# A two-stage attention kernel: the first part's order written out as one list, and the masks of stage 2 made early

## The chip, the core and the metric

The kernel runs on one core of a Trainium2 chip. The time is device time in microseconds (us), the slowest core of an execution, here the only one. A profiled execution is one more run, with the hardware profiler on; its span goes from the first to the last instruction of the core.

## What is computed

`reference.py`, cut to what matters. Two attentions follow each other, and the output of the first, regrouped by token, is the input of the second:

```python
# stage 1: q, k, v are (8 batches, 8 heads, 576 tokens, 64)
mask = (rel >= 0) & (rel < 64)                  # rel = query position - key position
attn = softmax(where(mask, q @ k.T / 8, -1e9))
x = (attn @ v), heads side by side: (8, 576, 512)
# stage 2: 4 experts, each a causal attention with 64 columns; 2 of 4 chosen per token
logits = x @ w_gate; keep the two largest, softmax over these two -> w
out = sum over the experts e kept of  w_e * (softmax(causal(x wq_e (x wk_e).T / 8)) @ (x wv_e)) @ wo_e
```

All arrays are f32. The products with the weights are formed from two reduced-precision parts (a high and a low one, names ending in `hi` and `lo`, `xh` and `xl`), three matmuls for one.

## The kernel before

**Stage 1.** Heads are taken in pairs `p`, 32 in all, four to a batch. A pair has nine blocks of 64 queries, and each block sees two blocks of 64 keys. Four blocks make a group `g`, so there are 72 groups, nine to a batch. For a group the steps are these:

- `s1_mm` (L201): scores on TensorE (PE) for two groups at once, 32 small matmuls, into two banks of PSUM (tag `s`, five banks). Text and names below call the call for groups 6 and 7 `m6`, and so on.
- `s1_qk`: the window mask and the row minimum on VectorE (DVE, L223), the exponentials on ScalarE (ACT, L231), then "norm": an add and a reciprocal on DVE (L238, L239) and four multiplications on GpSimd (POOL, L242), which leave the tile `sm`.
- `s1_t`: four transposes on PE (L262) for each group into a bank of PSUM (tag `t`, three banks), then the "evict", a copy of the bank to `pt` by ACT (L270) or DVE (L268). From group 18 on it is two groups to a bank, and DVE multiplies with a triangle (`tri`, L282) while it copies.
- `s1_av` (L303): 32 matmuls with `v` into a bank of tag `t`, whose result goes out as `xh` (ACT, L315) and `xl` (DVE, L317).

Text below writes t_3 for the transposes of group 3, sm_3 for its tile, o_3 for the 32 matmuls that end with group 3.

**Stage 2**, per batch: `s2_v` (`v2ps`, five products, with the copy of the logits at L415), the key and query projections (`kps`, `qps`; the matmuls are L384 to L386), the scores (L521), a masked softmax (DVE L542, ACT L546), transposes (L606, and L628 for the tile `px`, in the same three banks `t`), the product with `v` (L667), the output product (`ops`) and its copies (L710). It needs constants: `causal` and `m_f` (masks), `QF`, `V2` and `below` (tiles that must be cleared), all made in `stage2_constants`. The weights are loaded by `load_weight` and cut in two by `split_weights` (POOL the high part, DVE the low one).

**Loads** are all issued by SyncE (SP): `load_pair` (L86, L87) brings `q` and `k` of a pair, `load_v` (L99) brings `v`, each with three buffers; for pair 3 `q`, `k` and `v` go to the tiles `P2` (printed as `p`).

**What sets the order.** Every engine works off its instructions in the order in which they were emitted. Each step has a time on a scale of batches, and a heap hands the steps out by it. Steps with a time below `EARLY` (1.0) are emitted phase by phase: a step that yields goes back into the heap with a `DELAY` added. In this first part the order on PE, DVE, ACT and POOL is as emitted. After it, up to a time of 15.5, PE alone is held to the emitted order, and a scheduler of the framework orders the others; the order on SP is the framework's throughout.

Of the kernel before, what the change touches and what calls it, by code (L numbers as in the profile page):

```python
# [20 lines left out]
E = 4  # L21
DM = NH * D
NEG = -1.0e9
MERGE = 1
LPOS = (-2.607, -1.75, -1.7, -1.032, -2.6)
EARLY = 1.0
TPOS = 0.667
EPOS = {'V': (-0.113, 0.691), 'G': (1.179, 0.889), 'KQ0': (0.544, 0.987), 'KQ1': (-0.225, 0.85)}
ELAG = (0.453, 0.719)
EQ = (0.041, 0.024, 0.109, -0.306, -0.038, -0.309, 0.065, 0.065, -0.032, 0.149, 0.044, -0.017, -0.056, -0.019, -0.04, -0.032, -0.134, -0.038)  # L30
ET = (0.023, 0.156, -0.265, 0.001, 0.065, -0.095, 0.275, 0.092, 0.073, -0.065, 0.19, 0.023, 0.204, -0.256, 0.124, -0.171, -0.135, -0.241)
EV = (-0.045, 0.508, 0.147, 0.282, 0.083, 0.211, -0.168, 0.146, 0.096, 0.061, 0.442, 0.055, 0.456, 0.018, 0.112, -0.053, -0.034, -0.252)
DELAY = {'ttr': 0.008, 'exp': 0.04, 'norm': 0.193, 'evict': -0.227, 'xh': -0.02, 'xl': 0.181, 'v': 0.087, 'k': 0.008, 'lo': 0.343}
MM0 = 0.07
MORE = 0.0
MERGED = ()
MPOS = (0.091, 0.05)
WHOLE = ('sA1yb0xkt','sA1yb0xCkt')
LAG = (-0.048, 0.009, 0.29)
POS = {'T00': (-0.096, 0.044), 'T01': (-0.139, -0.078), 'T10': (0.181, 0.783), 'T11': (0.226, 0.424), 'T1l': (0.283, 0.638), 'O0': (0.161, 0.571), 'O1': (1.027, 0.988), 'KQ1': (-0.098, 0.991), 'V': (-0.003, 0.559), 'G': (0.685, 0.902), 'KQ0': (0.636, 0.932), 'VT': (-0.056, 0.001), 'T00e': (-0.05, 0.0), 'T10e': (0.096, 0.082), 'T01e': (-0.758, -0.894), 'T11e': (-0.421, -0.074), 'O0e': (0.418, 0.518), 'O1e': (0.851, 0.917)}  # L40
SPREAD = 'APAP'
LEAD = 12.49
FIXED = (1.0, 15.5)
WPOS = [-0.711, -0.311, 0.131, 0.616]
CPOS = 0.058
JOIN8 = 1
JOIN = 2
BPOS = ((0.044, 0.828), (0.147, 0.721), (0.08, 0.3, 0.203), (-0.511, 0.073))
# [10 lines left out]
def window_attention_moe_attention(ctx: ExitStack, tc: tile.TileContext, qT, kT, vW,  # L59
                                   wg, wq, wk, wv, wo, out):  # L60
    nc = tc.nc
# [10 lines left out]
    def need(*keys):  # L72
        assert made.issuperset(keys), keys
# [76 lines left out]
    raws = {}  # L150
# [94 lines left out]
    def s1_t(g):  # L245

        k = g % 9
        if k % 2 == 0 and k != 8:
            return
        gs = [g - 1, g] if k % 2 else [g]  # L250
        need(*(("p1", y) for y in gs))
        if k == 8 and g // 9 >= JOIN and JOIN8:
            t = work.tile([128, 2, 2, 128], F32, tag="pt8", bufs=1, name=f"pt1_{g}")
        else:
            t = work.tile([128, 4, 2, 128], F32, tag="pt1", bufs=2, name=f"pt1_{g}")
        if g < FIRST:
            banks = []
            for x, y in enumerate(gs):
                pt = P1.pop(y)
                ps = psum.tile([128, 4, 128], F32, tag="t", bufs=3, name=f"t1_{y}")  # L260
                for i in range(4):
                    nc.tensor.transpose(ps[:, i], pt[:, i], ident)  # L262
                banks.append(ps)
            yield "evict"
            for x, ps in enumerate(banks):
                dst = t[:, 2 * x:2 * x + 2].rearrange("r a e c -> r (a e) c")
                if gs[x] % 2 and gs[x] < 9:
                    nc.vector.tensor_copy(dst, ps)  # L268
# [60 lines left out]
    L = [const.tile([128, 5, E], F32, name=f"logits{i}") for i in range(2)]  # L329
# [5 lines left out]
    V2 = [const.tile([128, 5, E, D], F32, name=f"v2_{i}") for i in range(2)]  # L335
# [15 lines left out]
    def stage2_constants():  # L351
        made.add("late")
        nc.vector.memset(m_f, 0.0)
        for h in range(2):
            r = slice(64 * h, 64 * h + 64)
            nc.gpsimd.affine_select(out=m_f[r, 0:64], in_=m_f[r, 0:64], pattern=[[-1, 64]],
                                    base=0, channel_multiplier=1, compare_op=OP.is_ge, fill=NEG)

        nc.gpsimd.memset(causal, 0.0)
        for c in (0, 640):  # L360
            nc.gpsimd.memset(causal[0:64, c:c + 64], -NEG)
            nc.vector.tensor_scalar(causal[64:128, c:c + 64], m_f[64:128, 0:64], -1.0, None, op0=OP.mult)
        for c in (64, 576):
            nc.vector.tensor_scalar(causal[0:64, c:c + 64], m_f[0:64, 0:64], -1.0, None, op0=OP.mult)
        nc.vector.tensor_scalar(m_f[:, 64:128], m_f[:, 0:64], -1.0, None, op0=OP.mult)
        for t in QF:
            nc.gpsimd.memset(t, 0.0)
        for t in V2:
            for e in range(E):
                nc.gpsimd.memset(t[64 - 64 * (e % 2):128 - 64 * (e % 2), 4, e], 0.0)  # L370
        nc.gpsimd.memset(below, 0.0)
        for e in range(1, E):
            nc.gpsimd.memset(below[:, e, 0:e], 1.0)

# [346 lines left out]
    def half(n):  # L721
# [75 lines left out]
    todo = [x for n in range(2 * NB + 2) for x in half(n)]  # L797
    joined = {}
    places = []
    for n in range(1, 2 * NB + 2):  # L800
# [4 lines left out]
        for x in range(3 if n == 2 * NB else 2):  # L805
            t = n + BPOS[n - 2 * NB + 2 if n >= 2 * NB else (n + 1) % 2][x]
# [3 lines left out]
    for g in range(NG1):  # L810
        t = (g - LEAD - MORE * min(max(g - 9, 0) / 27, 1)) / 4.5 + LAG[0]
        a, c = (ELAG if t < EARLY - 0.5 else (2 / 4.5 + LAG[1], 3 / 4.5 + LAG[2]))
        if g < 18:
            t, a, c = t + EQ[g], a + ET[g] - EQ[g], c + EV[g] - EQ[g]
        base = t
        if g < SOLO:
            todo.append((t - 1e-4, s1_mm, ((g,),)))
        elif g % 2 == 0:
# [3 lines left out]
            if at_burst:  # L822
                t = places.pop(0)
# [16 lines left out]
    todo.append((CPOS, stage2_constants, ()))  # L840
    todo.append((max(WPOS[:3]) + DELAY['lo'] + 1e-3, clear_pt2, ()))
    todo += [(LPOS[i], load_weight, (i,)) for i in range(4)]
    todo += [(LPOS[4] + 1e-3 * p, load_v, (p,)) for p in (2, 3)]
    todo.append((-99, first_constants, ()))
    todo.append((TPOS, tri_constants, ()))

    def steps(f, args):
        r = f(*args)
        if r is not None:
            yield from r  # L850

    order = [(x[0], i, steps(*x[1:])) for i, x in enumerate(todo)]
    heapq.heapify(order)
    E_ = mybir.EngineType
    for t1, engines in ((EARLY, {E_.PE, E_.DVE, E_.Activation, E_.Pool}), (FIXED[0], None), (FIXED[1], {E_.PE}), (99, None)):
        with tc.manual_schedule(engines=engines) if engines else nullcontext():
            while order and order[0][0] < t1:
                t, i, unit = heapq.heappop(order)
                for phase in unit:
                    if t < EARLY:  # L860
                        heapq.heappush(order, (t + DELAY[phase], len(todo) + i, unit))
                        break


# [52 lines left out]
```

## Time and profile before

| | us |
|---|---|
| median of three runs (483.93, 484.5, 555.47) | 484.5 |
| profiled execution | 487.01 |
| its span | 485.0 |
| PE busy | 464.4 (96%) |
| DVE busy | 390.3 (80%) |
| ACT busy | 339.2 (70%) |
| POOL busy | 210.3 (43%) |
| mean granted clock of PE | 0.987 |

A busy share is an average over the whole span. The first part, the first 60 us or so, differs from the rest: there the loads from memory are the densest, and the idle time of PE is at its largest. The first part goes from the first score matmul to the first scores of stage 2 at 58.07 us; after it come eight batches of stage 2, among which the remaining groups of stage 1 are spread.

### The profile page before, as it was taken

The numbers are of one execution on the slowest core, as the hardware profiler recorded it, in microseconds if no ns is written. First come the engines' busy times: TensorE is split into PE (matmuls) and PEld (weight loads), VectorE is DVE, ScalarE is ACT, GpSimd is POOL, SyncE is SP. The second block draws the span as 40 slices with busy tenths as digits, with TensorE's granted clock in tenths as the row PEclk, the third lists the DMA queues.
The fourth block names the chain that finished last, engine by engine and source line by source line (L and its number), as shares of the span: only waits on it lengthen the run. The fifth ranks groups of instructions, "written<-read, shape, count | busy, mean of one in ns | idle before, by whom it ended". The sixth has DMA issues, their size and how long they took to land.

```text
span 485.0 us, 15973 instructions
## 1 busy us (share of the span) xinstructions
PE 464.4 (96%) x5728; PEld 416.3 (86%) x5728; DVE 390.3 (80%) x1758; ACT 339.2 (70%) x1349; POOL 210.3 (43%) x559
## 2 busy tenths in 40 slices
PE   6899999999999999999999999999899999999996
PEld 5678888997899898897889989898789989999875
DVE  3596789899978998888988998888997896646473
ACT  4796698948677874867668786576867785557480
POOL 3479955624254353441636244361436333242120
PEclk8799999999999999999999999999999999999999
DMA  8982243321623134123522214333240101200103
GB/s 275 389 300 85 89 144 110 103 82 47 220 97 103 51 123 130 64 98 102 201 90 88 91 49 173 118 101 102 78 141 23 51 1 47 66 2 23 66 2 108
DMA packets 20926, 51.36 MB, mean 106 GB/s; under 512 B 2800, under 2 KB 3824, under 8 KB 20848
## 3 DMA queue, kind: packets, MB, share of 16 engines
q1 hardware_dynamic: 20768, 50.22, 30.7%
q8 instruction: 45, 0.74, 0.7%
q14 instruction: 33, 0.27, 0.2%
q10 hardware_dynamic: 80, 0.13, 0.1%
HBM read 40.90 MB, written 9.44 MB: 104 GB/s over the span
## 4 chain that ended last, share of the span: by engine, by line
PE 46%; DVE 30%; ACT 17%; issue 4%; POOL 1%; DMA 1%; DVEq 0%; ACTq 0%; SPq 0%; POOLq 0%
DVE pt L282 8%; ACT p L231 6%; PE o L667 6%; ACT p L546 5%; PE o L303 4%; PE s L521 4%; PE s L201 4%; DVE sm L223 4%; DVE p L542 4%; PE t L606 4%; PE ops L386 2%; PE ops L384 2%; PE ops L385 2%; PE qps L384 2%; PE t L262 2%
## 5 line engine op out<-in xcount | busy, mean ns | idle before, releaser
L586 POOL TENSOR_SCALAR p<-p,r 128x192 f32<-128x192 f32 (+3 forms) x124 | 74.8, 620 | 86.8 <-DVE r L581 66.1
L546 ACT ACTIVATE p<-p,r 128x192 f32<-128x192 f32 (+3 forms) x128 | 77.3, 606 | 44.7 <-DVE r L566 31.6
L242 POOL TENSOR_SCALAR p<-p,st 128x64 f32<-128x64 f32 x216 | 64.4, 323 | 81.4 <-DVE st L239 57.5
L231 ACT ACTIVATE p<-p,st 128x64 f32<-128x64 f32 x216 | 72.8, 339 | 30.7 <-DVE p L228 16.8
L282 DVE TENSOR_TENSOR pt<-t,tri 64x512 f32<-64x512 f32 (+1 forms) x120 | 76.0, 634 | 2.0
L601 ACT ACTIVATE pt<-t 128x512 f32<-128x512 f32 (+3 forms) x185 | 66.5, 386 | 7.3 <-PE t L628 4.3
L223 DVE CUSTOM_DVE_ANT_0 sm<-s,win 128x128 f32<-128x128 f32 x264 | 62.8, 284 | 6.7 <-PE s L201 6.3
L542 DVE CUSTOM_DVE_ANT_0 p<-s,causal 128x320 f32<-128x320 f32 (+3 forms) x160 | 66.9, 471 | 0.9
L606 PE MATMUL t<-ident,p 128*128 128x128 f32 x384 | 55.3, 275 | 4.7 <-ACT pt L601 3.7
L606 PEld LDWEIGHTS t<-ident,p 128*128 128x128 f32 x384 | 43.7, 141 | 9.6 <-ACT pt L601 5.7
L667 PE MATMUL o<-pt,v 128*64 128x128 f32 (+3 forms) x896 | 51.1, 263 | 0.0
L201 PE MATMUL s<-k,q 64*64 64x128 f32 (+1 forms) x1116 | 43.7, 281 | 6.0 <-DVE st L238 2.6
L667 PEld LDWEIGHTS o<-pt,v 128*64 128x64 f32 x896 | 46.2, 137 | 2.0 <-issue 0.8
L201 PEld LDWEIGHTS s<-k,q 64*64 64x64 f32 x1116 | 33.4, 138 | 13.1 <-issue 5.8
L521 PE MATMUL s<-kt,qt 64*128 64x256 f32 (+2 forms) x480 | 44.4, 321 | 0.0
L303 PEld LDWEIGHTS o<-pt,v 128*64 128x64 f32 x1116 | 35.9, 140 | 6.3 <-issue 2.0
L303 PE MATMUL o<-pt,v 128*64 128x64 f32 x1116 | 40.4, 227 | 0.8 <-DVE pt L268 0.8
L231 ACT ACTIVATION_READ_ACCUMULATOR p<-p,st 128x1 f32 x216 | 40.8, 189 | 0.0
L384 PE MATMUL qps<-xh,wqhi 128*128 128x320 f32 (+1 forms) x128 | 40.5, 316 | 0.0
L384 PE MATMUL v2ps<-wvhi,xh 128*128 128x260 f32 x128 | 39.0, 304 | 1.6 <-DVE logits L415 1.0
L384 PE MATMUL kps<-xh,wkhi 128*128 128x320 f32 (+1 forms) x128 | 39.3, 307 | 0.0
L521 PEld LDWEIGHTS s<-kt,qt 64*128 64x128 f32 x480 | 34.6, 185 | 4.4 <-issue 0.4
(138 smaller groups left out, 1190.9 us busy)
## 6 DMA issues: line engine op xcount, KB each, us to landing
v<-in_vW_dram SPq DMA_DIRECT2D x31, 576.0 KB, 4.8
k<-in_kT_dram SPq DMA_DIRECT2D x30, 320.0 KB, 3.9
q<-in_qT_dram SPq DMA_DIRECT2D x30, 288.0 KB, 3.1
out_dram<-out SPq DMA_DIRECT2D x32, 256.0 KB, 2.0
out_dram<-out SPq DMA_DIRECT2D x7, 128.0 KB, 2.3
p<-in_vW_dram SPq DMA_DIRECT2D x1, 576.0 KB, 8.0
pt<-in_wv_dram SPq DMA_DIRECT2D x1, 512.0 KB, 9.1
pt<-in_wk_dram SPq DMA_DIRECT2D x1, 512.0 KB, 7.4
```

The source lines that it names most:

```text
L201: nc.tensor.matmul(S1[g][i][o:o + 64, c:], lhsT=q_t[r, 64 * b:64 * b + 64], rhs=k_t[r, 64 * b + c:64 * b + 128], start=True, stop=True)
L223: nc.vector.tensor_tensor_reduce(out=to, in0=ps[i][:, c:], in1=win[:, int(b == 0), c:], scale=-0.125, scalar=3.0e38, op0=OP.add, op1=OP.mi ...
L231: nc.scalar.activation(pt[:, i], pt[:, i], AF.Exp, bias=st[:, 0, z + i:z + i + 1], scale=-1.0, accum_out=st[:, 1, z + i:z + i + 1])
L282: nc.vector.tensor_mul(t[64 * w:64 * w + 64, :n, e], ps[r, :n], tri[r, w, None, :].to_broadcast([64, n, 128]))
L303: nc.tensor.matmul(o[64 * h:64 * h + 64, 4 * x + i], lhsT=pairs[p][2][:, h, b], rhs=t[:, i, c:c + 64], start=True, stop=True)
L384: nc.tensor.matmul(ps, lhsT=ah, rhs=bh, start=first, stop=False)
L521: nc.tensor.matmul(banks[e][:, at(i, e):at(i, e) + n], lhsT=QT[pr][r, w, q], rhs=rhs, start=x == 0, stop=x == 2)
L542: nc.vector.tensor_tensor_reduce(out=dst, in0=ps, in1=mask, scale=1.0, scalar=3.0e38, op0=OP.add, op1=OP.min, accum_out=to)
L546: nc.scalar.activation(p, p, AF.Exp, bias=r2[:, 0, x:x + 1], scale=-1.0, accum_out=r2[:, 1, x:x + 1])
L586: engine.tensor_scalar(p, p, r2[:, 3, x:x + 1], 1.0, op0=OP.mult, op1=OP.mult)
L606: nc.tensor.transpose(ps[:, col:col + 128], P2S[pr][part][:, at:at + 128], ident)
L667: nc.tensor.matmul(o[64 * h:64 * h + 64, q0:q0 + w], lhsT=V2[b % 2][:, c, 2 * pr + h], rhs=PT2[part][:, h, x:x + w], start=a == 0, stop=a ...
```

## The change

The steps below time 1.0 are no longer handed out by the heap. A string `ORDER` lists them by short names, and each occurrence of a name emits the next phase of that step on all four engines: `m` is `s1_mm`, `q` `s1_qk`, `t` `s1_t`, `a` `s1_av`, `l` and `L` the loads of weights and of `v`, `w` `split_weights`, `v`, `k`, `r` the first projections of stage 2, `f`, `c`, `d`, `e`, `i`, `z` the constants. `stage2_constants` (`c`) keeps `m_f` and `causal` alone; `clear_stage2` (`d`) has the rest but for the second `V2`, which `clear_v2` (`e`) clears later. `ECOPY` says which groups' banks DVE copies: group 3's goes from DVE to ACT. Some numbers of the tables `TPOS`, `EPOS` and `POS` change as well, which moves a few steps after the first part. No step is added or left out.

```diff
...
-CPOS = 0.058
+WPOS = (-0.711, -0.211, 0.131, 0.616)
+CPOS = (-1.5, -1.4, 0.7)
+ECOPY = (0, 1, 0, 0, 0, 1, 0, 1, 0, 0, 0, 0, 0, 0, 0, 0, 0, 0)
...
+ORDER = (
+    'f m0 q0 q0 q0 l0 L2 m1 q1 q0 q1 t0 q1 m2 q1 q2 q3 a0 t2 q2 L3 q2 q3 q3 t1 q2 m4 t1 q3 q5 q4 q4 q4 t3 '
+    'q5 c a1 l2 q4 q5 t3 a2 t4 a1 m6 q6 m8 q6 q5 l1 a1 t5 q6 q7 q7 q7 q6 t5 a3 a3 a4 q7 q8 d q8 a3 q8 l3 '
+    'a6 m10 q9 q9 q9 q8 t6 t7 t7 q10 a5 a5 q10 t8 t8 t9 q11 q10 a7 a7 a8 a8 w0 q9 a5 w0 q10 a7 w1 q11 a8 '
...
-POS = {'T00': (-0.096, 0.044), 'T01': (-0.139, -0.078), 'T10': (0.181, 0.783), 'T11': (0.226, 0.424), 'T1l': (0.283, 0.638), 'O0': (0.161, 0.571), 'O1': (1.027, 0.988), 'KQ1': (-0.098, 0.991), 'V': (-0.003, 0.559), 'G': (0.685, 0.902), 'KQ0': (0.636, 0.932), 'VT': (-0.056, 0.001), 'T00e': (-0.05, 0.0), 'T10e': (0.096, 0.082), 'T01e': (-0.758, -0.894), 'T11e': (-0.421, -0.074), 'O0e': (0.418, 0.518), 'O1e': (0.851, 0.917)}
+POS = {'T00': (-0.096, 0.053), 'T01': (-0.139, -0.078), 'T10': (0.181, 0.783), 'T11': (0.226, 0.424), 'T1l': (0.283, 0.638), 'O0': (0.161, 0.571), 'O1': (1.027, 0.955), 'KQ1': (-0.098, 0.991), 'V': (-0.003, 0.559), 'G': (0.684, 0.813), 'KQ0': (0.636, 0.963), 'VT': (-0.037, 0.001), 'T00e': (-0.05, 0.0), 'T10e': (0.096, 0.082), 'T01e': (-0.758, -0.894), 'T11e': (-0.421, -0.074), 'O0e': (0.418, 0.518), 'O1e': (0.851, 0.917)}
...
-                if gs[x] % 2 and gs[x] < 9:
+                if ECOPY[gs[x]]:
                     nc.vector.tensor_copy(dst, ps)
...
         nc.vector.tensor_scalar(m_f[:, 64:128], m_f[:, 0:64], -1.0, None, op0=OP.mult)
+
+    def clear_stage2():
         for t in QF:
             nc.gpsimd.memset(t, 0.0)
-        for t in V2:
-            for e in range(E):
-                nc.gpsimd.memset(t[64 - 64 * (e % 2):128 - 64 * (e % 2), 4, e], 0.0)
         nc.gpsimd.memset(below, 0.0)
         for e in range(1, E):
             nc.gpsimd.memset(below[:, e, 0:e], 1.0)
+        clear_v2(0)
+
+    def clear_v2(x):
+        assert x == 0 or not {"o"} & set(raws)
+        for e in range(E):
+            nc.gpsimd.memset(V2[x][64 - 64 * (e % 2):128 - 64 * (e % 2), 4, e], 0.0)
...
-    for t1, engines in ((EARLY, {E_.PE, E_.DVE, E_.Activation, E_.Pool}), (FIXED[0], None), (FIXED[1], {E_.PE}), (99, None)):
+    with tc.manual_schedule(engines={E_.PE, E_.DVE, E_.Activation, E_.Pool}):
+        for x in ORDER.split():
+            next(units[x], None)
+    for t1, engines in ((FIXED[0], None), (FIXED[1], {E_.PE}), (99, None)):
         with tc.manual_schedule(engines=engines) if engines else nullcontext():
             while order and order[0][0] < t1:
-                t, i, unit = heapq.heappop(order)
-                for phase in unit:
-                    if t < EARLY:
-                        heapq.heappush(order, (t + DELAY[phase], len(todo) + i, unit))
-                        break
+                for phase in heapq.heappop(order)[2]:
+                    pass
```

The first place is DVE after the copy of `pt_1`, about 13 us into the span. `st_3` is what the norm of group 3 works on, `sm_4` and `sm_5` are the mask steps of groups 4 and 5. Before:

```order
43 L268 COPY pt_1_248<-t_1_254 128x512
44 L223 ISA sm_4_284,st_4_283<-s_4_0_261,win 128x128
...
51 L223 ISA st_4_283 128x1
52 L238 TENSOR_SCALAR st_3_232<-st_3_232 128x4
53 L239 RECIPROCAL st_3_232<-st_3_232 128x4
54 L223 ISA sm_5_300,st_5_299<-s_4_0_261,win 128x128
```

With the change:

```order
43 L277 COPY pt_1_242<-t_1_248 128x512
44 L247 TENSOR_SCALAR st_3_232<-st_3_232 128x4
45 L248 RECIPROCAL st_3_232<-st_3_232 128x4
46 L232 ISA sm_4_290,st_4_289<-s_4_0_259,win 128x128
...
61 L232 ISA st_5_310 128x1
62 L362 MEMSET m_f 128x128
63 L371 TENSOR_SCALAR causal<-m_f 64x64 x2
64 L373 TENSOR_SCALAR causal<-m_f 64x64 x2
65 L374 TENSOR_SCALAR m_f<-m_f 128x64
66 L247 TENSOR_SCALAR st_4_289<-st_4_289 128x4
67 L248 RECIPROCAL st_4_289<-st_4_289 128x4
```

The norm of group 3 has moved ahead of sm_4's eight instructions, and the mask instructions of stage 2, which stood behind the split of `wk`, now stand between sm_5 and the norm of group 4. On POOL their partners stand between sm_3 and sm_4, and the clearing of `qf`, `below` and the first `V2` between sm_7 and sm_8.

The second place is PE after t_3. Before:

```order
29 L262 MATMUL t_3_322<-ident,sm_3_233 128x128 x4
30 L201 MATMUL s_6_0_336<-k_84,q_83 64x128 x2
...
38 L303 MATMUL o_1_370<-pt_1_248,v_81 64x64 x16
39 L262 MATMUL t_4_389<-ident,sm_4_284 128x128 x4
40 L262 MATMUL t_5_394<-ident,sm_5_300 128x128 x4
41 L303 MATMUL o_3_418<-pt_3_316,v_81 64x64 x2
42 L303 MATMUL o_3_418<-pt_3_316,v_87 64x64 x14
43 L201 MATMUL s_8_0_438<-p_0_67,p_1_68 64x128 x2
```

With the change:

```order
29 L271 MATMUL t_3_305<-ident,sm_3_233 128x128 x4
30 L312 MATMUL o_1_333<-pt_1_242,v_81 64x64 x16
31 L210 MATMUL s_6_0_364<-k_84,q_83 64x128 x2
...
39 L210 MATMUL s_8_0_386<-p_0_67,p_1_68 64x128 x2
...
47 L271 MATMUL t_4_419<-ident,sm_4_290 128x128 x4
48 L271 MATMUL t_5_424<-ident,sm_5_311 128x128 x4
49 L312 MATMUL o_3_451<-pt_3_299,v_81 64x64 x2
```

o_1 has gone ahead of m6, and m8 (`s_8`) from behind o_3 to ahead of t_4. The second half of m8 reads pair 4. On SP the load of pair 3's `v` (576 KB) goes from ahead of pair 4's `q` and `k` to behind them.

The third place is PE in each batch of stage 2, at the query projection of the second half (`qps_0_1`). Before:

```order
467 L606 MATMUL t_0_1_0_1_1953<-ident,p_0_67 128x128 x4
468 L384 MATMUL qps_0_1_1961<-xh_863,wqhi 128x256
469 L385 MATMUL qps_0_1_1961<-xl_864,wqhi 128x256
...
479 L386 MATMUL qps_0_1_1961<-xh_863,wqlo 128x256
480 L628 MATMUL t_0_1_0_2_1976<-ident,px 128x128
```

With the change:

```order
467 L620 MATMUL t_0_1_0_1_1953<-ident,p_0_67 128x128 x4
468 L642 MATMUL t_0_1_0_2_1961<-ident,px 128x128
469 L398 MATMUL qps_0_1_1965<-xh_890,wqhi 128x256
470 L399 MATMUL qps_0_1_1965<-xl_891,wqhi 128x256
...
480 L400 MATMUL qps_0_1_1965<-xh_890,wqlo 128x256
```

One transpose, that of `px`, has gone ahead of the twelve matmuls of the projection. It writes a bank of tag `t` that the triangle step (L282) on DVE read last.

## Rows read from the trace of the kernel before

**Rows 1.** The page: busy time of two engines, their share, instructions.
```profile
PE 464.4 (96%) x5728; PEld 416.3 (86%) x5728; DVE 390.3 (80%) x1758; ACT 339.2 (70%) x1349; POOL 210.3 (43%) x559
```

**Rows 2.** What PE waited for, 0 to 62 us: total, times, longest.
```profile
PE s L201 <- DVE st L238: 2.6, 1, 2.6
PE t L262 <- POOL sm L242: 1.4, 2, 1.2
...
PE v2ps L384 <- DVE logits L415: 1.0, 1, 1.0
PE o L303 <- DVE pt L268: 0.8, 1, 0.8
PE t L262 <- DVE xl L317: 0.4, 1, 0.4
```

**Rows 3.** Stretches: length, busy us per engine, granted PE clock, DMA share, GB/s.
```profile
18.00:20.00 2.00, 2.00 (x37) 1.55 (x39) 1.24 (x4) 1.11 (x5) 1.60 (x5) 0.68 1.05 396
20.00:22.00 2.00, 2.00 (x34) 1.88 (x33) 0.86 (x8) 1.74 (x9) 1.11 (x4) 0.50 1.04 402
```

**Rows 4.** PE's timeline: start, us, line, tiles, count, [idle before, releaser].
```profile
16.93 1.37 PE L262 MATMUL t<-ident,sm 128*128 128x128 f32 x4 [1.21 <-POOL sm L242]
...
19.73 1.97 PE L303 MATMUL o<-pt,v 128*64 128x64 f32 x32
...
25.84 1.15 PE L303 MATMUL o<-pt,v 128*64 128x64 f32 x32
...
30.23 0.88 PE L262 MATMUL t<-ident,sm 128*128 128x128 f32 x4
```

**Rows 5.** DVE's timeline around the norm of group 3 and the masks.
```profile
13.12 0.66 DVE L268 COPY pt<-t 128x512 f32<-128x512 f32 x1
15.11 0.29 DVE L223 CUSTOM_DVE_ANT_0 sm<-s,win 128x128 f32<-128x128 f32 x1 [1.33 <-PE s L201]
...
15.96 0.16 DVE L238 TENSOR_SCALAR st<-st 128x4 f32<-128x4 f32 x1
16.16 0.18 DVE L239 RECIPROCAL st<-st 128x4 f32<-128x4 f32 x1
...
42.56 0.62 DVE L362 TENSOR_SCALAR causal<-m_f 64x64 f32<-64x64 f32 x2 [3.51 <-POOL causal L359]
...
43.41 0.18 DVE L365 TENSOR_SCALAR m_f<-m_f 128x64 f32<-128x64 f32 x1
```

**Rows 6.** ACT's timeline: the end of group 3's exponentials.
```profile
14.14 0.19 ACT L231 ACTIVATION_READ_ACCUMULATOR sm<-sm,st 128x1 f32 x1
```

**Rows 7.** POOL's timeline: groups 3 and 4, and the stage 2 constants.
```profile
16.50 2.80 POOL L242 TENSOR_SCALAR sm<-sm,st 128x128 f32<-128x128 f32 x8 [1.72 <-DVE st L239]
...
41.25 0.53 POOL L356 TENSOR_SCALAR_AFFINE_SELECT m_f<-m_f 64x64 f32<-64x64 f32 x2
...
42.76 0.34 POOL L367 MEMSET qf<- 128x128 f32 x2
43.16 1.45 POOL L370 MEMSET v<- 64x64 f32 x8
```

**Rows 8.** Loads of `k` issued from 13 to 16 us, and how long until landing.
```profile
L87 SPq DMA_DIRECT2D k<-in_kT_dram x2: 328/328/328, 13.5 to 15.1; - x2
...
DMA to landing us min/median/max: 7.6/7.6/7.7
```

**Rows 9.** What PE waited for, 62 to 485 us.
```profile
PE t L606 <- ACT pt L601: 3.7, 6, 1.0
PE s L201 <- DVE out L710: 1.9, 3, 0.6
PE t L606 <- DVE xl L317: 0.9, 3, 0.3
```

**Rows 10.** PE's timeline where the first second-half query projection starts.
```profile
101.60 0.37 PE L384 MATMUL qps<-xh,wqhi 128*128 128x256 f32 x1
```

**Rows 11.** DVE's timeline at the same place.
```profile
100.50 1.40 DVE L282 TENSOR_TENSOR pt<-t,tri 64x512 f32<-64x512 f32 x2
```

More of the change, by code (lines that the diff above doesn't have):

```diff
@@ L24 @@
 MERGE = 1
-LPOS = (-2.607, -1.75, -1.7, -1.032, -2.6)
+LPOS = (-2.607, -1.75, -1.7, -0.983, -2.6)
 EARLY = 1.0
[L27 to L33, printed above, removed]
+ORDER = (
[6 rows of a table added]
+)
+TPOS = 0.589
+EPOS = {'V': (-0.113, 0.518), 'G': (1.179, 0.889), 'KQ0': (0.544, 0.89), 'KQ1': (-0.225, 0.85)}
+ELAG = (0.433, 0.719)
+EQ = (0.041, 0.024, 0.109, -0.306, -0.038, -0.309, 0.065, 0.065, -0.032, 0.149, 0.044, -0.017, 0.046, -0.006, -0.04, -0.032, -0.134, -0.038)
+ET = (0.014, 0.139, -0.265, 0.001, 0.065, -0.084, 0.275, 0.092, 0.081, -0.065, 0.208, 0.023, 0.238, -0.256, 0.124, -0.171, -0.135, -0.241)
+EV = (-0.045, 0.353, 0.147, 0.282, 0.083, 0.211, -0.168, 0.146, -0.059, -0.073, 0.536, 0.055, 0.456, 0.018, 0.096, -0.053, -0.037, -0.252)
+DELAY = {'ttr': 0.024, 'exp': 0.04, 'norm': 0.183, 'evict': -0.227, 'xh': -0.02, 'xl': 0.181, 'v': 0.087, 'k': 0.008, 'lo': 0.343}
 MM0 = 0.07
@@ L43 @@
 FIXED = (1.0, 15.5)
-WPOS = [-0.711, -0.311, 0.131, 0.616]
-CPOS = 0.058
+WPOS = (-0.711, -0.211, 0.131, 0.616)
+CPOS = (-1.5, -1.4, 0.7)
+ECOPY = (0, 1, 0, 0, 0, 1, 0, 1, 0, 0, 0, 0, 0, 0, 0, 0, 0, 0)
 JOIN8 = 1
@@ L361, in stage2_constants @@
             nc.gpsimd.memset(causal[0:64, c:c + 64], -NEG)
+        for c in (0, 640):
             nc.vector.tensor_scalar(causal[64:128, c:c + 64], m_f[64:128, 0:64], -1.0, None, op0=OP.mult)
@@ L839, in window_attention_moe_attention @@
     todo += [(WPOS[i], split_weights, (i,)) for i in range(4)]
-    todo.append((CPOS, stage2_constants, ()))
+    todo.append((CPOS[0], stage2_constants, ()))
+    todo.append((CPOS[1], clear_stage2, ()))
+    todo.append((max(CPOS[2], WPOS[3] + DELAY['lo'] + 1e-3), clear_v2, (1,)))
     todo.append((max(WPOS[:3]) + DELAY['lo'] + 1e-3, clear_pt2, ()))
@@ L850, in steps, with name @@
             yield from r
+    short = dict(s1_mm="m", s1_qk="q", s1_t="t", s1_av="a", split_weights="w", load_weight="l", load_v="L", s2_v="v",
+                 s2_gate="g", s2_k="k", s2_q="r", stage2_constants="c", tri_constants="i", clear_pt2="z",
+                 first_constants="f", clear_stage2="d", clear_v2="e")
+    def name(f, args):
+        if f is s1_mm:
+            return f"m{args[0][0]}"
+        return short.get(f.__name__, f.__name__) + "".join(map(str, args))
     order = [(x[0], i, steps(*x[1:])) for i, x in enumerate(todo)]
+    units = {name(*x[1:]): order[i][2] for i, x in enumerate(todo)}
     heapq.heapify(order)
     E_ = mybir.EngineType
-    for t1, engines in ((EARLY, {E_.PE, E_.DVE, E_.Activation, E_.Pool}), (FIXED[0], None), (FIXED[1], {E_.PE}), (99, None)):
+    with tc.manual_schedule(engines={E_.PE, E_.DVE, E_.Activation, E_.Pool}):
+        for x in ORDER.split():
+            next(units[x], None)
+    for t1, engines in ((FIXED[0], None), (FIXED[1], {E_.PE}), (99, None)):
         with tc.manual_schedule(engines=engines) if engines else nullcontext():
             while order and order[0][0] < t1:
-                t, i, unit = heapq.heappop(order)
-                for phase in unit:
-                    if t < EARLY:
-                        heapq.heappush(order, (t + DELAY[phase], len(todo) + i, unit))
-                        break
+                for phase in heapq.heappop(order)[2]:
+                    pass
 _OUTS = [((8, 576, 512), 'float32')]
```

3 rows, old and new, of the table ORDER are left out of this document.

## The prediction

> **What bounds the kernel now.** I read the page first. PE is busy for 464.4 of 485.0 us and DVE for 390.3 [rows 1]: whatever the change does, at most some 20 us of PE's span can be won, and only where PE stands still. So the next view is what PE waits for, in two parts. Up to 62 us [rows 2] the reader sees one long wait, 2.6 us (the first keys have to land), and then four short ones that stand in the way of the change: 1.2 us for sm_3 from POOL, 0.8 for a copied bank, 1.0 for the logits of `v2ps`, 0.4 for `xl`. After 62 us [rows 9] PE waits for six evicts (3.7 in all), three output copies (1.9) and three `xl` (0.9).
>
> Two more views tell how those short waits come about. In the timelines DVE stands still for 1.33 us before it takes up sm_4 [rows 5], while the norm of group 3, which is in line behind sm_4, has had its exponentials since 14.33 (14.14 + 0.19, [rows 6]). And DVE stands for 3.51 us in front of the first `causal` instruction, because POOL comes to the masks only at 41.25 [rows 5, 7]; the copy of the logits and with it PE's `v2ps` are in line behind that. [...]
>
> **The change, part by part.**
>
> *Norm of group 3 ahead of sm_4.* Add and reciprocal took 0.38 us (15.96 to 16.34), and POOL began 0.16 later [rows 5, 7]. From 14.33 they end at 14.71, in the gap in which DVE did nothing, so DVE pays nothing. POOL starts at 14.87; its eight multiplications took 2.80, four take 1.40, so sm_3 is whole at 16.27 instead of 17.90. t_3 followed POOL's pace and was over at 18.30 (16.93 + 1.37) [rows 4], 0.4 after POOL; now about 16.6. That is **1.7 us earlier**.
>
> *o_1 ahead of m6, m8 ahead of t_4.* PE then has o_1 (its copy of `pt` ended at 13.78, [rows 5]) and m6, 1.15 us each at full clock as an estimate from the L303 row of that count: to about 18.9. m8 wants pair 4. Of the two keys issued at 13.5 and 15.1, which landed 7.6 and 7.7 us later [rows 8], the first is pair 4's: 21.1. Pair 3's `v` now comes behind it; at 396 GB/s [rows 3] its 590 kB take 1.5 us, so pair 4 lands at 19.6. m8's second half waits about 0.5 us and ends near 20.5. Matmuls that stood after o_3 are thus done in the time in which PE waits for sm_4.
>
> *Masks (`c`) between sm_3 and sm_4.* On POOL the four rows of `m_f` and `causal` took 1.5 us (41.25 to 42.76, [rows 7]); with sm_3 over at 16.3 and `m_f` set by DVE at 17.0, POOL is through at 18.5. DVE's part took 1.03 us (42.56 to 43.59, [rows 5]), so to 19.5, and the norm of group 4 queued behind it is done at 19.9. sm_4 is made from 20.1 to 21.5 and sm_5 to 22.9, t_5 ends at 23.0 and o_3 at 24.1. Nothing else queues there on DVE that PE wants sooner. By 24.1 PE has done what it had done at 25.84 before [rows 4], m8 with it: **1.7 us ahead** still. Up to here it doesn't matter at which clock m6 and m8 ran: POOL sets the pace.
>
> *`clear_stage2` (`d`) between sm_7 and sm_8.* On POOL 0.34 for `qf`, half of 1.45 for one `V2`, and some 0.3 for `below` [rows 7], 1.4 us in all. sm_8 comes that much later, but PE has m10, t_6, t_7 and o_5 ahead of t_8. In my count t_8 ends at 28.8 to 29.1; it ended at 31.11 (30.23 + 0.88) [rows 4]. The 0.4 us for `xl` [rows 2] goes too: **2.0 to 2.3 us ahead**.
>
> *Masks gone from the later place.* The 3.51 us of DVE, and PE's 0.95 for the logits behind it, have no cause left [rows 2, 5]. DVE gets time there, and what then comes last is the split of the weights and the copies of `v2ps`, which PE must in part wait for all the same: I count 0.3 to 0.95. First part in all: 2.3 to 3.1 us, I take **2.6**. Its ends: the four waits that can go make 1.2 + 0.8 + 1.0 + 0.4 = 3.4 us [rows 2], the upper end; the lower is 0.5, if later groups wait for DVE and ACT, which have the same work as before.
>
> *`wk` loaded behind `wq`, group 3's evict on ACT.* Weights are wanted from 30 us on, so a load 2.7 us later (512 KB and 576 KB at that rate) is hidden by the work of groups 6 to 12. The evict takes no time off the path: o_3 reads it only after t_5.
>
> *The transpose of `px` ahead of `qps_0_1`.* PE comes to this place at 101.60 [rows 10], and the last L282 of the run, which reads the bank that `px` gets, ends at 101.90 (100.50 + 1.40) [rows 11]. The twelve matmuls covered that; now PE waits 0.3 us with the matmuls queued behind. I find the same pattern six times, so at most 1.9 us. The waits that come later in each batch, 0.3 to 1.0 us each [rows 9], are for other engines and shrink when PE is later. I take **0.5 us** lost, with 0 and 1.9 as ends. The output products that go ahead of a transpose at odd batches could cover the three waits for `xl` (0.9, [rows 9]); I count nothing, since `xl` is not needed sooner than before.
>
> *Sum.* -2.6 + 0.5 = -2.1. Against the profiled execution's own 487.0 this gives 484.9; its span is 485.0, with 2.0 around it that the change doesn't touch. The median shown is 484.5, 2.5 less than the profiled time, so **482.4**.
>
> [...] Beside t_2 to t_5, eight plus eight transposes with waits between them, the clock falls [rows 3]. [...]
>
> **The rivals.**
>
> *A, more.* All four waits go (3.4) and the three for `xl` with them (0.9), and the six banks come free in time: -4.3, **480.2**. For it: three of the four are for an engine that had stood idle shortly before (POOL 1.72 us, DVE 1.33 and 3.51) [rows 5, 7]. Against: sm_4 and sm_8 get POOL work ahead of them.
>
> *B, given back.* The low stretch moves from m6 and o_1 to o_3, m10 and what follows, where PE and not POOL sets the pace. 3.3 us at half speed do the work of 1.65; 2.6 - 1.65 - 0.5 leaves 0.5, **484.0**. If instead the six bank waits count in full, 2.6 - 1.9 leaves 0.7, nearly the same. For it: about 1 us of PE's time between 20.5 and 23.0 is idle in my count, much as the 1.21 before the fall that rows 3 and 4 show.
>
> *C, slower.* The mask step becomes what DVE stands for, earlier than before and with all of stage 1 behind it: the norms of groups 4 and 5, `xl_1` and sm_6. It decides if POOL reaches the masks later than about 18.5 instead of 17.0. Then sm_4 ends at 23.0, o_3 at 25.6, no lead is left, the low clock follows as in B (1.65) and `d` adds its 1.4 before sm_8, less the 0.95 saved later: +2.1, with the bank waits +0.5: **487.1**. For it: DVE did stand 3.51 us there [rows 5]. Against: POOL was idle for 1.72 us before sm_3 [rows 7] and DVE for 1.33.
>
> That the change does nothing is not a case: the orders of PE, DVE and POOL differ at the places named.
>
> **How the numbers follow.** Forecast 0.48 (its own range 481.4 to 484.2, from 3.1 won and nothing lost, to 0.8 won and 0.5 lost), A 0.18, B 0.22, C 0.10, other 0.02. The range should leave out C's far half, what lies beyond A, and the rest: **479.4 to 485.8**. A change of 2%, 9.7 us, is about what a measurement of this kernel can tell from none; all the cases lie within it, so faster 0.02, same 0.95, slower 0.03, the small ones for what I did not see.
>
> **What would show it.** In the changed profile: PE's wait for sm_3 at 16 us down from 1.2 to some 0.7; sm_3 on POOL from 14.9; m8 waiting about 0.5 us for a key; DVE's wait for POOL's `causal` below 1.5 us and near 17 us; no wait for the logits near 43 us; first scores of stage 2 about 2.6 us earlier; a wait at the `px` transpose near 99, six times, for DVE L282. Wrong would be: a low clock from 23 us on (B), a wait for sm_4 above 2 us (C), or first scores of stage 2 that come within 1 us of where they were, which would mean that DVE and ACT, not the order, set the pace of the first part.

## The result: 479.3 us, a gain of 1.0%, two and a half times the forecast

| | before | changed |
|---|---|---|
| median, us (runs) | 484.78 (4) | 479.34 (4) |
| profiled execution, us | 487.01 | 480.83 |
| span, us | 485.0 | 478.8 |
| mean granted clock | 0.987 | 0.993 |
| ratio, 95% interval | | 0.9899 [0.9867, 0.9931] |

The forecast was 482.4 in a range of 479.4 to 485.8. The sign was right and the size was not: 2.1 us were forecast, and 5.4 lie between the medians, which puts the result at the very edge of the range. The two traces differ by 6.2, because the profiled run of before stood 2.2 above its median and that of the change 1.5. The profiled execution of before was one of its long ones: of 19 runs of that kernel beside an experiment below, four had a mean granted clock of 0.989 and took 487.1 to 487.5 us, the others 0.994 to 1.000 and 483.2 to 485.7.

The first scores of stage 2 tell how the 6.2 us are divided. In both traces PE has done the same 678 matmuls ahead of them. The row is that of the first projections' key tile, of the changed kernel: durations in ns, then first and last start.

```profile
L535 PE MATMUL s<-kt,qt x18: 276/306/381, 53.1 to 54.4; 64*128 64x256 f32 x6, 64*128 64x320 f32 x6, 64*128 64x448 f32 x6
```

At 58.1 before, 53.1 now: 5.0 us in the first part and 1.2 after it. These are two single executions. With the same list another trace below has its first scores at 51.35, and with the old first part another has them at 57.13; the medians of the experiments divide the gain as 3.9 and 1.4. What PE waits for in the first part, of the changed kernel, beside [rows 2]:

```profile
PE s L210 <- DMA k<-in_kT_dram: 5.7, 3, 3.3
PE warm L133 <- DVE px L128: 1.1, 1, 1.1
PE t L271 <- ACT pt L279: 0.6, 1, 0.6
PE t L271 <- POOL sm L251: 0.2, 1, 0.2
```

All four waits that the prediction counted as removable are gone; the longest ones left are for keys from memory. The longest, 3.3 us, stands where [rows 2] has 2.6 with a label of DVE: it is for the keys of the rest of m2, and in the trace of the list alone no wait at that place is above 0.2 us. The next is m8's. PE's timeline of the changed kernel, with the two stretches around it:

```profile
15.03 2.02 PE L271 MATMUL t<-ident,sm 128*128 128x128 f32 x8
16.98 1.15 PE L312 MATMUL o<-pt,v 128*64 128x64 f32 x32
...
21.75 0.67 PE L210 MATMUL s<-k,q 64*64 64x128 f32 x16 [2.15 <-DMA k<-in_kT_dram]
22.34 1.09 PE L271 MATMUL t<-ident,sm 128*128 128x128 f32 x8
```

t_3 ends at 17.05 (18.30 before, [rows 4]); m8 waits 2.15 us for pair 4's key, where 0.5 was forecast. The granted clock (third number from the right) of the same stretches, beside [rows 3]:

```profile
16.00:18.00 2.00, 1.94 (x36) 1.43 (x35) 1.17 (x11) 2.00 (x12) 1.29 (x5) 1.00 1.04 392
18.00:20.00 2.00, 1.60 (x54) 1.30 (x48) 1.39 (x12) 2.00 (x8) 1.14 (x4) 1.00 1.04 401
20.00:22.00 2.00, 0.25 (x8) 0.26 (x12) 1.97 (x14) 2.00 (x11) 2.00 (x7) 1.00 1.03 393
22.00:24.00 2.00, 2.00 (x45) 1.66 (x38) 0.94 (x5) 1.77 (x9) 1.92 (x6) 1.00 1.05 393
```

The low stretch of [rows 3] is not there in this trace, though PE is busy for only 0.25 of the 2 us from 20 on. Both traces have an earlier one that [rows 3] doesn't show and that begins within that wait for m2's keys: the granted clock is 0.50 from 8.5 to 15.3 us before and from 7.9 to 14.7 with the change. One stretch of it, before and changed:

```profile
12.00:14.00 2.00, 2.00 (x25) 1.67 (x28) 1.68 (x11) 2.00 (x12) 0.63 (x2) 0.50 1.06 388
```

```profile
12.00:14.00 2.00, 2.00 (x19) 1.67 (x21) 1.90 (x15) 2.00 (x11) 0.30 (x1) 0.50 1.05 381
```

DVE's place for the masks, beside [rows 5]:

```profile
18.56 0.30 DVE L371 TENSOR_SCALAR causal<-m_f 64x64 f32<-64x64 f32 x2 [1.39 <-POOL causal L367]
```

After the first part, what PE waits for, beside [rows 9]:

```profile
PE t L620 <- ACT pt L615: 3.4, 5, 1.0
PE s L210 <- DVE out L724: 2.0, 3, 0.7
PE t L642 <- DVE pt L291: 1.3, 6, 0.2
PE s L210 <- PE s L210: 0.2, 1, 0.2
```

The six waits at the `px` transpose are there, 0.2 us each, 1.3 in all. The three for `xl` (0.9) are not.

### The profile page after: what moved, and what is told of

Same layout as the page of the kernel before. It is cut to its first block, busy times and chain, and to the rows that moved or that the text cites. A ratio compares the mean times of both kernels' runs of the same rounds, so it can differ in the third digit from the quotient of the medians.

```text
span 478.8 us, 15973 instructions
## 1 busy us (share of the span) xinstructions
PE 459.5 (96%) x5728; PEld 413.3 (86%) x5728; DVE 387.6 (81%) x1757; ACT 340.2 (71%) x1350; POOL 210.8 (44%) x559
## 4 chain that ended last, share of the span: by engine, by line
PE 40%; DVE 31%; ACT 16%; DMA 5%; issue 4%; POOL 2%; SPq 1%; DVEq 0%; ACTq 0%; POOLq 0%
DVE pt L291 11%; ACT p L560 7%; ACT p L240 6%; PE o L681 6%; DVE p L556 5%; PE s L535 5%; PE o L312 4%; DVE sm L232 4%; DMA k<-in_kT_dram 4%; PE t L620 3%; DVE out L724 2%; PE s L210 2%; PE qps L398 2%; PE ops L400 2%; PE ops L398 2%
```

## Experiments

All times are medians of five rounds, against before on the same chip (484.5 to 484.8 each time).

### Which half: the list alone, the later moves alone

The changed kernel with the old `POS` and `EPOS`; and the kernel of before with the new `POS`. The new `EPOS` is in neither.

```diff
-POS = {'T00': (-0.096, 0.053), ... 'O1': (1.027, 0.955), ... 'KQ0': (0.636, 0.963), 'VT': (-0.037, 0.001), ...
+POS = {'T00': (-0.096, 0.044), ... 'O1': (1.027, 0.988), ... 'KQ0': (0.636, 0.932), 'VT': (-0.056, 0.001), ...
```

> The changed kernel with the old numbers of POS and EPOS: the written list alone, and after it the order of before. Theory 1 (the first part gained 5.0 us, as the two traces show at the first scores of stage 2, and the rest 1.2): 480.0, between 479.4 and 480.8, first scores of stage 2 near 53.1 us, no wait at the px transpose, three waits for xl of about 0.3 us. Theory 2 (the prediction's terms; 2.6 in the first part, and the rest from other things): 482.0.

> The kernel of before with the new POS: only the moves after the first part. Theory 1 (the waits for xl and the bank waits at even batches go, the px waits are made up at the next wait): 483.4, between 482.9 and 484.2, six px waits of about 0.2 us. Theory 2 (the prediction's term): 485.0, half a microsecond slower than before. First scores of stage 2 at 58 us by both.

Measured: the list alone 480.7, ratio 0.9912 [0.9887, 0.9936]; the later moves alone 483.22, ratio 0.9968 [0.9951, 0.9984]. 3.9 and 1.4 add up to the whole, within the intervals. So the later moves are a gain, where the prediction had a loss of 0.5. The list alone has its first scores at 51.35 us, 1.7 earlier than the changed kernel's trace with the same list. The waits after 62 us with the list alone, where PE has the order of before:

```profile
PE t L620 <- ACT pt L615: 3.6, 6, 1.0
PE s L210 <- DVE out L724: 1.9, 3, 0.7
PE t L620 <- DVE xl L326: 0.9, 3, 0.3
PE v2ps L398 <- DVE r L556: 0.7, 2, 0.4
PE s L210 <- DVE r L556: 0.6, 2, 0.3
```

The `xl` row and the two `r` rows are what the new numbers take away. `v2ps` waits for a bank that DVE's softmax step reads; at even batches the change puts six output products (`ops_4`) ahead of `v2ps_4`, which the prediction did not weigh at all. That this move is what takes the `v2ps` waits away is not shown by itself. In the trace of the later moves alone the first two `px` places lose about 0.4 us each against before, and a later wait that is no longer there returns it. At the first one the lead over before is 0.95 us ahead of the place, 0.55 behind it, and 0.99 at the next transposes, where before waited for `xl`. At the second it falls from 1.01 to 0.62 and comes back only at a `v2ps`, some 40 us later.

In the list's own trace pair 4's key came in time, and m8's wait is the forecast 0.5:

```profile
19.08 0.67 PE L210 MATMUL s<-k,q 64*64 64x128 f32 x16 [0.50 <-DMA k<-in_kT_dram]
```

### The masks: late in the new order, early in the old one

In the list, `c` and `d` go back behind `w1`'s second mention, the split of `wk`: both, `c` alone, `d` alone.

```diff
-    '... t3 q5 c a1 l2 ... q7 q8 d q8 a3 ... m14 v01 w1 q14 ...'
+    '... t3 q5 a1 l2 ... q7 q8 q8 a3 ... m14 v01 w1 c d q14 ...'
```

> The changed kernel with the mask step and clear_stage2 put back behind the split of wk in the list. Theory 1 (the masks and clears on POOL and DVE held the logits, and sm_13 and sm_14 behind them, for about 2 us together): 481.2, between 480.6 and 482; the wait for the logits of about 1 us is back, and t_13, t_14 take 2 us instead of 1.0. Theory 2 (only the wait for the logits, and the early masks cost nearly as much before sm_4 and sm_8): 479.3 to 479.9.

> The changed kernel with the mask step alone (c: m_f and causal, on POOL and on DVE) put back behind the split of wk; the clears (d) stay early. Theory 1 (DVE, standing for POOL's masks with the logits and the norms behind it, carries the loss of 5.7 us that c and d together showed): 483.5, between 482.5 and 484.5, with a wait for the logits of 2.5 us or more. Theory 2 (POOL is the engine that has no time between 30 and 57 us, so that any work there costs about its own length): 481.0 to 481.8, as c is 1.5 to 1.7 us of POOL.

> The changed kernel with the clears alone (d: qf, below and the first V2, 1.4 us on POOL, nothing on DVE) put back behind the split of wk; the masks stay early. Theory 1 (the loss is DVE's standing for the masks): 479.3 to 479.8, hardly any loss. Theory 2 (POOL has no time there): 480.5 to 481, about 1.4 us more than the changed kernel. The prediction's count (clears early delay sm_8 by 1.4 us): 478.9 or a little less, a gain.

And in the kernel of before, heap and all, the masks alone go early, cut in three as in the change:

```diff
-CPOS = 0.058
+CPOS = (-1.5, -1.4, 0.7)
...
-    todo.append((CPOS, stage2_constants, ()))
+    todo.append((CPOS[0], stage2_constants, ()))
+    todo.append((CPOS[1], clear_stage2, ()))
+    todo.append((max(CPOS[2], WPOS[3] + DELAY['lo'] + 1e-3), clear_v2, (1,)))
```

> The kernel of before, its heap and its numbers, with the mask step and the clears alone moved early, to where the heap puts them by the change's CPOS (behind the norm of group 5, ahead of sm_6), and the second V2 cleared at the end. Theory 1 (what 3.6 us of POOL and 3.5 of DVE cost between 39 and 58 us is about 2.9 us, and the early place costs 0.5 to 1.5): 482.8, between 482 and 483.6, first scores of stage 2 near 56 us. Theory 2 (the prediction's term, 0.3 to 0.95, and the early place costs as much): 484.2 to 485.

Measured: both late 485.04, ratio 1.0007 [0.9987, 1.0027], above both theories of that run; `c` alone late 484.9, 1.0011 [0.9994, 1.0029]; `d` alone late 479.2, 0.9898 [0.9873, 0.9923]; masks early in the old order 485.83, 1.0032 [1.0013, 1.0050].

`c` alone takes back the whole gain, more than either theory had it, and `d` nothing. What PE waits for with `c` late, then DVE's timeline, then a stretch behind it:

```profile
PE kps L398 <- DVE logits L429: 3.9, 1, 3.9
```

```profile
42.57 0.30 DVE L371 TENSOR_SCALAR causal<-m_f 64x64 f32<-64x64 f32 x2 [3.91 <-POOL causal L367]
```

```profile
46.00:48.00 2.00, 2.00 (x26) 1.67 (x26) 1.08 (x2) 2.00 (x9) 2.00 (x4) 0.50 0.00 0
```

DVE stands 3.91 us for POOL, the logits are queued behind, PE stands as long, and the granted clock, 1.00 from 38 to 44 us, is then 0.50 from 46 to 48. `d` puts 1.4 us on POOL in the same place and no cost shows, so it is not POOL's time there that is dear but DVE's standing. The theory that POOL has no time to give falls.

How long PE takes from m14's first matmul to the first scores of stage 2 measures the place by itself. Of before, of the change, of `c` late, of `d` late and of the masks early in the old order:

```profile
37.77 0.45 PE L201 MATMUL s<-k,q 64*64 64x128 f32 x8
58.07 0.39 PE L521 MATMUL s<-kt,qt 64*128 64x256 f32 x2
```

```profile
35.65 0.56 PE L210 MATMUL s<-k,q 64*64 64x128 f32 x12
53.06 0.38 PE L535 MATMUL s<-kt,qt 64*128 64x256 f32 x2
```

```profile
35.37 0.89 PE L210 MATMUL s<-k,q 64*64 64x128 f32 x24
58.39 0.39 PE L535 MATMUL s<-kt,qt 64*128 64x256 f32 x2
```

```profile
34.08 0.67 PE L210 MATMUL s<-k,q 64*64 64x128 f32 x16
51.49 0.38 PE L535 MATMUL s<-kt,qt 64*128 64x256 f32 x2
```

```profile
37.77 0.45 PE L201 MATMUL s<-k,q 64*64 64x128 f32 x8
55.63 0.39 PE L527 MATMUL s<-kt,qt 64*128 64x256 f32 x2
```

20.3 before, 17.4 changed, 23.0 with `c` late, 17.4 with `d` late, 17.9 with the masks early in the old order. PE does the same 228 matmuls in between, and the other traces agree: 20.3 in both other kernels with the old order, 23.2 with both late, 17.4 in the other kernels with the list. So the masks' going is worth 2.4 us there with the old order kept and 5.6 in the list; from the old order to the change it is 2.9. By the rows the 5.6 are PE's 3.9 of standing and some 1.7 of low clock behind it (an estimate from the 0.91, 0.50 and 0.74 granted from 44 to 50 us).

In the old order the 2.4 us are lost again and more, and both theories of that run were too hopeful. At the early place (waits of PE, then of DVE):

```profile
PE o L303 <- DVE pt L268: 1.7, 1, 1.7
```

```profile
DVE causal L363 <- POOL causal L359: 2.7, 1, 2.7
```

The heap puts POOL's masks behind sm_5, DVE stands 2.7 us for them, and the copy of group 3's bank is queued behind: o_3 waits, 0.96 us longer than before, and the clock then falls to 0.50 from 24 to 26 us. Behind the first scores this trace takes 428.0 us and that of before 426.9; why is not known. In the list POOL has the masks ahead of sm_4, DVE stands 1.4 us, and ACT does that copy. The early masks pay only together with the list.

### The list's single moves

The norm of group 3 back behind sm_4 on DVE; group 3's copy back on DVE; m8 back behind t_4, t_5 and o_3.

```diff
-    '... t1 q3 q5 q4 q4 q4 t3 ...'
+    '... t1 q5 q4 q4 q3 q4 t3 ...'
```

```diff
-ECOPY = (0, 1, 0, 0, 0, 1, ...
+ECOPY = (0, 1, 0, 1, 0, 1, ...
```

```diff
-    '... c a1 l2 q4 q5 t3 a2 t4 a1 m6 q6 m8 q6 q5 l1 a1 t5 q6 q7 q7 q7 q6 t5 a3 a3 ...'
+    '... c l2 q4 q5 t3 a2 t4 a1 m6 a1 q6 q6 q5 l1 a1 t5 q6 q7 q7 q7 q6 t5 a3 m8 a3 ...'
```

In the last one the first two mentions of `a1` stand later in the list as well; that changes the order on no engine.

> The changed kernel with the norm of group 3 put back behind sm_4's mask step on DVE, and nothing else. Theory 1 (the prediction's first term: t_3 comes 1.7 us later; the wait of m8 for pair 4's key, half a microsecond or more, takes some of it, and the masks on POOL come as much later): 480.3, between 479.9 and 481; t_3 waits for POOL again. Theory 2 (pair 4's key sets the end of this place whatever t_3 does): 479.3.

> The changed kernel with group 3's bank copied by DVE again, in the list's place, which is behind the masks and the norm of group 4. Theory 1 (the copy is done near 20.3 us, ahead of o_3, as the prediction had it): 479.3 to 479.6. Theory 2 (the copy behind DVE's standing for the masks holds o_3, as it did for 1.7 us in the kernel with early masks in the old order): 480.3 or more, and a wait of o_3 for DVE.

> The changed kernel with m8 back behind t_4, t_5 and o_3 on PE; o_1 stays ahead of m6. Theory 1 (m8 fills PE's wait for sm_4; without it PE stands there and has m8's 1.1 us to do later): 480.2, between 479.9 and 480.6, a wait of t_4 for POOL of 1 us or more, none for pair 4's key. Theory 2 (m8's wait for the key costs as much as it fills): 479.3 or less.

Measured: 481.59, ratio 0.9927 [0.9901, 0.9953]; 480.29, 0.9903 [0.9872, 0.9934]; 480.17, 0.9906 [0.9879, 0.9933]. All three medians lie on the side of a loss, 2.2, 0.9 and 0.8 us from the changed kernel's, and all three intervals overlap its own. None is shown by itself. In the norm's trace t_3 waits 0.61 us for POOL, half of the 1.21 of before; its median lies above the range of either theory. With group 3's copy on DVE no wait of o_3 for it shows, though the time is that of theory 2. With m8 back, t_4 waits 0.84 us for ACT's `xh`, not for POOL as expected, and t_4 and t_5 take 2.77 us instead of 1.09.

### Pair 4's key first, and px back

The loads of `wv` and of pair 2's `v` (`l0 L2`) go behind `m2`, which puts pair 4's `q` and `k` ahead of them on SP; in a second kernel `KQ0`'s old number puts the `px` transpose back behind `qps_0_1` as well.

```diff
-    'f m0 q0 q0 q0 l0 L2 m1 q1 q0 q1 t0 q1 m2 q1 ...'
+    'f m0 q0 q0 q0 m1 q1 q0 q1 t0 q1 m2 l0 L2 q1 ...'
...
-'KQ0': (0.636, 0.963)
+'KQ0': (0.636, 0.932)
```

> The changed kernel with the loads of wv and of pair 2's v emitted behind those of pair 4, so that m8's key lands some 2.5 us sooner. Theory 1 (PE's wait of 2.15 us for that key stands beside the chain through the masks, sm_4 and sm_5 on POOL, which ends about 0.6 us before it): 478.8, a gain of 0.3 to 0.7 over the changed kernel, and t_4 waits for POOL. Theory 2 (the key alone sets this place): 477.3.

> The changed kernel with pair 4's load first and with KQ0's old number, which puts the px transpose back behind qps_0_1 and changes nothing else on PE. Theory 1 (each px wait delays PE by 0.4 us, and the waits for evicts and output copies that follow give it back): 479.0, within 0.3 of the same kernel with px ahead. Theory 2 (the six waits count): 477.7 (1.3 us of waits) or, with the transpose's own time, 476.6.

Measured: 479.03, ratio 0.9875 [0.9848, 0.9902]; with `px` back as well 478.57, 0.9884 [0.9855, 0.9913]. Neither differs from the changed kernel by more than the intervals, so no gain of either is shown. With the key in time, in the first kernel's trace, m8 doesn't wait for it, and t_4 and t_5 are paced by POOL's sm_4 and sm_5 instead:

```profile
19.61 2.07 PE L271 MATMUL t<-ident,sm 128*128 128x128 f32 x8
```

So an earlier key alone can win little here. Nor is a cost of the six `px` waits shown. The rows of the second kernel tell why: `px` behind brings `xl` and `r` back.

```profile
PE t L620 <- DVE xl L326: 0.8, 3, 0.3
PE s L210 <- DVE r L556: 0.6, 2, 0.3
```

### The low clock

The kernel of before with matmuls in PE's wait for sm_3.

```diff
+                for i in range(5 if y == 3 else 0):
+                    nc.tensor.matmul(ps[:, i % 4], lhsT=ident, rhs=ident, start=True, stop=True)
                 for i in range(4):
                     nc.tensor.transpose(ps[:, i], pt[:, i], ident)
```

> The kernel of before with five 128x128 matmuls of ident with itself, 1.2 us of PE, ahead of t_3's transposes into the same bank, where PE waits 1.2 us for sm_3; the transposes overwrite them. Theory 1 (PE's standing there, among transposes, is what brings the low clock from 18.7 us on, and that costs up to 1.7 us): no low stretch between 16 and 24 us, 483.2, between 482.8 and 483.8. Theory 2 (POOL and the loads set the pace there, so the clock costs nothing): 484.5, whatever the clock does.

Measured 483.75, ratio 0.9981 [0.9961, 1.0001]: about 1 us, at the edge of what the runs can tell. Stretches of its trace:

```profile
18.00:20.00 2.00, 1.22 (x16) 0.98 (x17) 0.98 (x4) 2.00 (x9) 0.47 (x2) 1.00 1.03 387
20.00:22.00 2.00, 2.00 (x68) 1.76 (x65) 1.41 (x9) 2.00 (x9) 0.36 (x2) 1.00 1.04 406
```

In this trace, with the wait filled, the granted clock is 1.00 in every stretch from 16 to 24 us, as theory 1 had it, and the gain is smaller than its 1.7 us. One trace does not show that filling the wait is what kept the clock up: the mean granted clock of the twelve runs was 0.992 to 1.000, and three of the 19 runs of before, with nothing filled, had 1.000 too. The later moves alone, with the old first part, fell to 0.50 from 18 to 20 us; the list alone showed 1.00 in every stretch from 16 to 26 us. But the list doesn't always keep 1.00 there. With `c` late, where the list is the changed kernel's up to that place but for the masks, m8 waited as long as in the changed kernel's trace (2.21 us, 2.15 there), and the clock did fall, to 0.50 from 22 to 24 us:

```profile
20.45 0.67 PE L210 MATMUL s<-k,q 64*64 64x128 f32 x16 [2.21 <-DMA k<-in_kT_dram]
21.05 1.34 PE L271 MATMUL t<-ident,sm 128*128 128x128 f32 x8
22.32 1.98 PE L312 MATMUL o<-pt,v 128*64 128x64 f32 x32
```

```profile
22.00:24.00 2.00, 2.00 (x34) 1.68 (x32) 1.53 (x10) 0.40 (x1) 0.99 (x4) 0.50 1.06 406
```

## Why the prediction was right in sign and short in size

- **Norm, o_1, m8.** t_3 was to end at 16.6 and o_3 at 24.1; they end at 17.05 and 24.52 in the changed trace, 16.03 and 22.82 with the list alone, where the key came in time. The order of events is the forecast's, but the term was too large. About half of the norm's 1.7 us came from one execution's clock: in the trace of before, m4 ran in the low stretch from 8.5 to 15.3 us (0.50) and took 1.99 us, DVE stood 1.33 for it ahead of sm_4, and the norm began 2.98 us behind m4's first matmul. With the masks early in the old order m4 took 1.10, as long as m10 in the changed kernel's trace at 1.00, DVE stood 0.28, the norm began 2.10 behind m4, and t_3 waited 0.71 for POOL instead of 1.21 (DVE, then PE):

```profile
12.74 0.29 DVE L223 CUSTOM_DVE_ANT_0 sm<-s,win 128x128 f32<-128x128 f32 x1 [0.28 <-PE s L201]
```

```profile
14.56 1.37 PE L262 MATMUL t<-ident,sm 128*128 128x128 f32 x4 [0.71 <-POOL sm L242]
```

  The forecast had the list 2.0 to 2.3 us ahead by t_8. At m14 the two traces are 2.1 apart, but the medians leave only about 1.0 for all that comes ahead of m14 (an estimate: 3.9 for the list alone less the 2.9 below), so that agreement is in part luck. Which single move carries it stays open: undoing them one at a time moved the time by 0.8 to 2.2 us, inside the intervals.
- **Masks early.** DVE's wait was to be below 1.5 us near 17 us: 1.39, beginning at 17.17. That the early place is cheap holds in the list alone; in the old order the move costs more than the late place gives (485.83).
- **Masks gone from the later place: the term that was mis-sized.** "I count 0.3 to 0.95". It is 2.9 us (20.3 against 17.4), 2.4 of it by the masks and clears alone. I counted the one labelled wait of PE, 0.95, and the idle time as its upper end. But PE's busy time also holds waits: t_13 and t_14, eight transposes that take 1.03 us in the changed kernel, took 2.15 before, because t_14 came as POOL finished sm_14. PE's timeline of before, and of the changed kernel:

```profile
51.72 0.60 PE L262 MATMUL t<-ident,sm 128*128 128x128 f32 x4
52.49 1.38 PE L262 MATMUL t<-ident,sm 128*128 128x128 f32 x4 [0.17 <-POOL sm L242]
```

```profile
46.41 1.03 PE L271 MATMUL t<-ident,sm 128*128 128x128 f32 x8
```

  The label says 0.17; four transposes take 1.38 instead of some 0.5. With the masks early in the old order the eight take 1.04 too, so it is the late place of the masks and clears that held sm_14. The two, 0.95 and 1.1, make 2.1 of the 2.9; most of the rest is t_11 and t_12, and m16, behind which the next matmul came 0.4 and 0.3 us later than in the changed kernel. The upper end of the first part, 3.4 us, had the same fault.
- **Low clock.** The forecast gave it no term of its own but as a loss (rival B), and its rows show the clock from 18 to 22 us, not the low stretch from 8.5 to 15.3. No run shows the 1.65 us that B and C count for 3.3 us at half speed. The trace of before has 0.50 from 18.7 to 22.1 us, in which 32 matmuls took 1.97 us against 1.15 at 1.00 [rows 4]; with `c` late, 0.94, 0.50 and 0.71 from 20 to 26 us, m8 came 1.30 us ahead of the changed kernel's and m14 0.28, so some 1.0 us went in between (an estimate; the masks on POOL differ too). How much of the gain is a low stretch that is gone stays open: filling the wait in the old order gave about 1 us, with an interval that reaches 1.
- **`clear_stage2`.** Counted as a delay of 1.4 for sm_8; no cost of either place shows (479.2 with `d` late).
- **After the first part: the sign was wrong.** 0.5 lost was forecast, 1.4 was won. The px waits came as forecast, six times, 0.2 us each and not 0.3, and are given back, which I had half foreseen. I counted nothing for the waits for `xl`, and thought that, if anything, the output products put ahead of a transpose would cover them. It is the `px` transpose's new place that does: where it alone went back, with the products' new places kept, the `xl` waits returned (0.8). And I left out the two waits of `v2ps`, which go as well.

So the sum came out near by errors of both signs: too much for the start, too little for the masks, the wrong sign for the end.

Of the rivals, A (all four waits and the `xl` ones go) came nearest in time, 480.2, and its rows are the changed kernel's but for the six bank waits, which stayed; but it reached that sum by labelled waits, and the rest came from paced transposes and perhaps the clock. B did not happen in the changed kernel's trace: t_4 and t_5 run together at 22.34 and the clock is 1.00 from 22 to 24 us. It did happen with `c` late, where t_4 and t_5 run together at 21.05, the clock is 0.50 from 22 to 24 us, and o_3 took 1.98 us and m10 1.53 (1.15 and 1.10 in the changed kernel's trace). So the same eight transposes behind m8's wait are followed by the low clock in one of these two traces and not in the other. Transposes in the filled gap were not tried, so it stays open whether they have a share in any fall. C, slower, is not what the change does; it is what the masks early in the old order do: DVE stands 2.7 us, o_3 is held, 485.83.

## What to carry to other kernels

An engine that stands for another with others' work queued behind it cost more here than the bound engine's labelled wait showed (2.9 us at the masks' later place against 0.95): also compare how long the same matmuls take from one fixed point to the next, since paced transposes count as busy (t_14's four 1.38 us instead of some 0.5). A step that is moved away from a bad place has to be given a good one on every engine that it uses; moved by itself, the mask step took its wait along (DVE 2.7 us at the early place, and 485.83). Price each reordered pair of steps by the wait that it covers (0.9 for `xl`) as well as by the one that it opens (1.3 at `px`). And before a wait of one profile is priced, see at which granted clock the work ahead of it ran in that execution (m4: 1.99 us at 0.50, 1.10 in another trace).

## What was not expected of the hardware

Pair 4's key, issued at 12.41 us, took 9.3 us to land in the changed kernel's trace, 9.3 with `c` late too, and 8.2 to 8.4 in others of the same load order (list alone, `d` late); the stretches of 2 us meanwhile moved 354 to 401 GB/s in the changed kernel's trace and 353 to 409 with the list alone. Why it took longer is not known. PE stood for 2.15 us from 19.6 us on and the granted clock was 1.00 from 18 to 26 us; with `c` late it stood for 2.21 us at the same place, and 0.50 followed from 22 to 24. Before, 1.21 us among transposes had been followed by 0.50 from 18.7 to 22.1. So the length of PE's standing alone does not tell these cases apart.
